# Expert 2's first layer split four slices later, and expert 0's low products three slices behind the high ones

## The chip, the cores and the metric

One core of one Trainium2 chip runs the kernel. The metric is the device time of one execution in microseconds (us); lower is better. The core has a matrix engine (TensorE, PE in the profile, its weight loads PEld), VectorE (DVE), ScalarE (ACT), GpSimd (POOL) and SyncE (SP), which work side by side, each through its own instructions in order, and 16 DMA engines.

## The reference

What is computed is an attention whose mask comes from hashed signs, followed by a layer of eight experts. Each token goes to the one expert with the largest gate logit:

```python
for i in range(N):                     # N = 1536 tokens of D = 512
    e = expert_idx[i]
    if counts[e] < capacity:           # capacity 384
        disp[e, counts[e]] = x[i]
        ...
h = np.maximum(np.einsum('ecd,edf->ecf', disp, w1), 0.0)   # w1: 8 x 512 x 1024
y = np.einsum('ecf,efd->ecd', h, w2)                       # w2: 8 x 1024 x 512
for i in range(N):
    if keep[i]:
        out[i] = gate_w[i] * y[expert_idx[i], pos[i]]
```

All of it is float32.

## The kernel before

The attention takes the first 250 us or so and isn't touched. After it the eight experts run one after another. An expert has up to two tiles of 128 tokens (more are dealt with in a branch behind a test, which is not taken in the execution profiled here). The hidden width of 1024 is cut into eight **slices** of 128, numbered f = 0 to 7.

To keep float32 accuracy on TensorE, each operand is split into a high part (rounded by ACT, names ending in h) and a low part (the rest, made by DVE, or for two slices by POOL, names ending in l). A product is then three matmuls: high by high, high by low, low by high. So each slice of a weight costs an ACT and a DVE instruction before its last matmul can run. `split1` and `split2` (by `split`, L1143 and L1144) do this for a slice of w1 and of w2, for the expert after the one that is being computed.

`layer1` (L1205) makes a slice of the hidden layer in 12 matmuls into one of three PSUM banks, in turn; `relu` (L1174 on ACT, L1175 on DVE) empties the bank into `hh` and `hl`; then it calls `each(f)`. So the fourth slice can't begin before the relu of the first has read its bank, and so on. `layer2` (L1222) adds up three matmuls for each slice and tile into one bank for each tile: `w2h` with `hh`, `w2l` with `hh`, `w2h` with `hl`, in this order, and calls `each(f)` after a slice. In the loop over the experts, `each1` (called in `layer1`) splits slice f of the next expert's w1 and, at odd f, loads a piece of two slices of the w1 of the expert after that; `each` (called in `layer2`) splits slice f of the next expert's w2, loads on, and at f = 3 turns the next expert's tokens with `prep_x` (transposes on PE at L1164, `xh` by ACT, `xl` by DVE).

Expert 0 is different. Its first tile is computed in `hidden` (raw float32, L178) between the last steps of the routing; its w2 is split by `split_hi` (ACT, L1244) and `split_lo` (DVE and POOL, L1250), and its hidden layer by `relu_hi` and `relu_lo` (L1260, L1264). Then come `layer2` for its first tile, in which `turn` (L1181) transposes its second tile after slice 6; `raw_layer1` (L178) for the second tile, during which expert 1's w1 (`r1x`) is split; and `layer2` for the second tile. From then on experts 1 to 7 follow.

What sets the order is the order in which this code is written: instructions go to each engine's queue as the code issues them, and each queue is worked through in that order. Loads of weights are issued on SP (`load_w1`, `load_w2`), those of expert 1's w1 and of most of its w2 on ACT's queue; gathers of tokens and scatters of results on POOL. A buffer of raw weights is loaded again when both parts of the split before it have been made.

Of the kernel before, what the change touches and what calls it, by code (L numbers as in the profile page):

```python
# [114 lines left out]
def hash_attention_moe(ctx, tc, qT, kT, vL, wg, w1, w2, cst, out, CAP):  # L115
    nc = tc.nc
# [37 lines left out]
    def load_w1(e, c):  # L154
        t = wr.tile([128, 2, 4, 128], F32, tag="r1", name=f"r1_{e}")
        nc.sync.dma_start(out=t, in_=w1[e, :, 2 * c:2 * c + 2])
        return t

    raw1, raw2, xg = {}, {}, {}
    def load_w2(e, c, t=None, q=nc.sync):  # L160
        raw2[e, c] = t or gp.tile([128, 2, 512], F32, tag="r2", name=f"r2_{e}", bufs=3)
        q.dma_start(out=raw2[e, c], in_=w2[e, :, 2 * c:2 * c + 2])
# [3 lines left out]
    def col(e, t):  # L166
        return NJ if t == 3 else 3 * e + t
# [945 lines left out]
    with tc.manual_schedule():  # L1113
# [16 lines left out]
        W1, W2 = {}, {}  # L1130

        def load_w1c(e, c):
            if e < E and (e, c) not in raw1:
                raw1[e, c] = load_w1(e, c)

        def next_w2(n):
            if n + 3 < 4 * E:
                load_w2(*divmod(n + 3, 4))
# [8 lines left out]
        def split1(e, f, eng=nc.vector):  # L1147
            W1[e, f] = split(raw1[e, f // 2][:, f % 2], "w1", eng)

        def split2(e, f, eng=nc.vector):  # L1150
            W2[e, f] = split(raw2[e, f // 2][:, f % 2], "w2", eng)

        def fetch(e, t):
            gather(e, t, gp.tile([128, XW], F32, tag="xr", name="xr"))

        def prep_x(e, t0, nt):
            W = 128 * nt
            xr = [xg.pop((e, t0 + t)) for t in range(nt)]
            xh = xp.tile([128, 4, W], F32R, tag="xh", name="xh")
            xl = xp.tile([128, 4, W], F32R, tag="xl", name="xl")  # L1160
            for t, x in enumerate(xr):
                pt = ps.tile([128, 4, 128], F32, tag=f"t{t}", name="pt")
                for k in range(4):
                    nc.tensor.transpose(pt[:, k], x[:, k * 128:(k + 1) * 128], ident)  # L1164
                c = slice(t * 128, (t + 1) * 128)
                nc.scalar.activation(out=xh[:, :, c], in_=pt, func=AF.Copy)
                nc.vector.tensor_tensor(out=xl[:, :, c], in0=pt, in1=xh[:, :, c].bitcast(F32), op=ALU.subtract)
            return xh, xl

        def new_h(W):  # L1170
            return [hp.tile([128, 8, W], F32R, tag=tag, name=tag) for tag in ("hh", "hl")]
# [14 lines left out]
        def raw_layer1(e, xt, each):  # L1186
            hh, hl = new_h(128)
            for f in range(8):
                ph = ps.tile([128, 512], F32, tag=f"h{f % 3}", name="ph")
                raw_one(ph[:, :128], e, f, xt, range(4))  # L1190
                relu(ph[:, :128], hh[:, f], hl[:, f])
                each(f)
            return hh, hl

        def layer1(e, xhl, each):
            xh, xl = xhl
            W = xh.shape[2]
            hh, hl = new_h(W)
            for f in range(8):
                ph = ps.tile([128, 512], F32, tag=f"h{f % 3}", name="ph")  # L1200
                wh, wl = W1.pop((e, f))
                n = 0
                for k in range(4):
                    for w, x in ((wh, xh), (wh, xl), (wl, xh)):
                        nc.tensor.matmul(ph[:, :W], w[:, k], x[:, k], start=(n == 0), stop=(n == 11))  # L1205
                        n += 1
                relu(ph[:, :W], hh[:, f], hl[:, f])
                each(f)
            return hh, hl

        def layer2(e, hhl, t0, view, each, steps, now=True):
            hh, hl = hhl
            late = []
            py = {}
            for f, ts in steps:
                wh, wl = W2[e, f]
                for t in ts:
                    if f == 0:
                        py[t] = ps.tile([128, 512], F32, tag=("y0", "acc")[t], name="py")
                    c = slice(t * 128, (t + 1) * 128)  # L1220
                    for n, (h, w) in enumerate(((hh, wh), (hh, wl), (hl, wh))):
                        nc.tensor.matmul(py[t], h[:, f, c], w, start=(f == 0 and n == 0), stop=(f == 7 and n == 2))  # L1222
                    if f == 7:
                        def fin(t=t):
                            y = yp.tile([128, 512], F32, tag="y", name="y")
                            j = col(e, t0 + t)
                            nc.scalar.activation(out=y, in_=py[t], func=AF.Copy, scale=gsc[:, j:j + 1])  # L1227
                            nc.gpsimd.indirect_dma_start(  # L1228
                                out=outv[view(t)], out_offset=bass.IndirectOffsetOnAxis(ap=yix[:, j:j + 1], axis=0),
                                in_=y, in_offset=None, bounds_check=out.shape[0] - 1, oob_is_err=False)  # L1230

                        if now:
                            fin()
                        else:
                            late.append(fin)
                each(f)
            return late
# [18 lines left out]
        h0 = new_h(128)  # L1256
# [44 lines left out]
        def each0(f):  # L1301
            if f == 6:
                last_gates(0)
                xg[0, 1, "T"] = turn(0, 1)

        fin = layer2(0, h0, 0, lambda t: 0, each0, [(f, (0,)) for f in range(8)], False)
        for c in range(3):
            load_w2(1, c, q=nc.scalar)

        def each1(f):  # L1310
            if f in (0, 3, 6):
                last_gates((0, 3, 6).index(f) + 1)
            if f == 4:
                fin[0]()
            split1(1, f)

        h1 = raw_layer1(0, xg.pop((0, 1, "T")), each1)
        both = [(f, (0, 1)) for f in range(8)]
        apart = [(f, (t,)) for t in range(2) for f in range(8)]
        nxt = {}  # L1320
        for e in range(E):
            more = e + 1 < E
            if more and e:
                fetch(e + 1, 0)
                fetch(e + 1, 1)

            def each1(f):
                if more:
                    split1(e + 1, f)
                    if f % 2 and e + 2 < E:  # L1330
                        load_w1c(e + 2, f // 2)

            if e:
                hhl = layer1(e, nxt.pop("xhl"), each1)

            def each(f):
                if more:
                    split2(e + 1, f)
                    if f % 2:
                        next_w2(4 * (e + 1) + f // 2)  # L1340
                    if e == 0 and f > 3:
                        load_w1c(2, f - 4)
                    if f == 3:
                        nxt["xhl"] = prep_x(e + 1, 0, 2)

            if e:
                layer2(e, hhl, 0, lambda t: 2 * e + t, each, both if more else apart)
            else:
                layer2(0, h1, 1, lambda t: 1, each, [(f, (0,)) for f in range(8)])
                nmax = nc.values_load(mcnt[0:1, 0:1], min_val=0, max_val=2 * S)  # L1350
        with tc.If(nmax > WB):
# [3 lines left out]
            for e in range(E):  # L1355
# [8 lines left out]
                for t in (2, 3) if e == 0 else (2,):  # L1364
                    kept = {f: W1[e, f] for f in range(8)}
                    fetch(e, t)
                    hhl = layer1(e, prep_x(e, t, 1), lambda f: None)
# [31 lines left out]
```

## Time and profile before

| | us |
|---|---|
| median of 3 runs | 459.41 (458.39 to 460.09) |
| the profiled execution | 457.68 |
| its span, first to last instruction | 455.80 |
| mean granted TensorE clock, as a share of 2.4 GHz | 0.972 |
| PE busy | 421.9 (93%) |
| DVE, ACT, POOL busy | 322.2, 304.3, 207.9 |

The profiled execution is 1.73 us below the median of the runs, and 1.88 us of it lie outside the span. All times of day below are us from the span's start. A row of a timeline gives an instruction's start, its duration, engine, line, operation, output and inputs, shape and count, and in brackets how long the engine sat idle before it and for whom it waited.

### The profile page before, as it was taken

The page shows a single profiled execution, that of the slowest core. Times are in us where ns is not written, and L with a number is a line of the kernel's source. Part 1 is how long each engine was busy: PE and PEld are TensorE (multiplying, and loading weights), DVE is VectorE, ACT ScalarE, POOL GpSimd, SP SyncE. Part 2 cuts the span into 40 slices and gives each one's busy share as a digit, 9 for nine tenths or more (in the row PEclk, how much of TensorE's full clock was granted, in tenths as well). Part 3 has the DMA queues.
Part 4 walks back from the last instruction along what each step waited for, and adds up shares of the span by engine and source line. Part 5 has one row for each costly group of instructions (what it writes and reads, how often), then busy time and mean ns, then how long its engine had stood idle before and what let it go on. Part 6 is the DMA issues. An engine that isn't in the chain of part 4 may idle for free. (4 is left out here: it accounts for less than half of the span.)

```text
span 455.8 us, 10104 instructions
## 1 busy us (share of the span) xinstructions
PE 421.9 (93%) x3891; PEld 359.5 (79%) x3891; DVE 322.2 (71%) x675; ACT 304.3 (67%) x467; POOL 207.9 (46%) x190
## 2 busy tenths in 40 slices
PE   7887999699989999899998999899999999999993
PEld 2565877488877887787887879789898989898982
DVE  3886899976887879899867478576657575756310
ACT  4278989679777989999893447556565665656310
POOL 7567666778785775586872330203030303030100
PEclk9998999889988999999989999999999999999997
DMA  8997989889978999998897894977676666751000
GB/s 204 268 204 141 187 179 216 204 180 156 213 156 165 174 199 180 185 227 181 163 143 185 288 327 152 364 264 242 204 230 223 217 231 205 248 174 47 36 1 33
DMA packets 98910, 86.59 MB, mean 190 GB/s; under 512 B 79266, under 2 KB 81282, under 8 KB 98856
## 3 DMA queue, kind: packets, MB, share of 16 engines
q1 hardware_dynamic: 95288, 74.87, 68.7%
q0 software_dynamic: 2560, 7.34, 4.8%
q10 hardware_dynamic: 1008, 3.67, 2.3%
q8 instruction: 32, 0.52, 0.5%
q14 instruction: 22, 0.18, 0.2%
HBM read 48.35 MB, written 7.34 MB: 122 GB/s over the span
## 5 line engine op out<-in xcount | busy, mean ns | idle before, releaser
L1228 POOL DMA_INDIRECT y<-y,yix x16 | 17.5, 1095 | 150.1 <-ACT y L1227 134.7
L692 POOL TENSOR_TENSOR p<-p,p 128x768 f16<-128x768 f32 x37 | 62.2, 1700 | 21.3 <-ACT p L778 14.5
L1205 PE MATMUL ph<-xh,w1h 128*128 128x256 f32 x224 | 63.6, 284 | 2.2 <-DVE hl L1175 2.2
L1205 PE MATMUL ph<-xl,w1h 128*128 128x256 f32 x224 | 63.4, 283 | 0.0
L1205 PE MATMUL ph<-xh,w1l 128*128 128x256 f32 x224 | 63.4, 283 | 0.0
L625 PE MATMUL pt<-KA,QA 128*128 128x512 f32 x192 | 59.0, 390 | 2.3 <-ACT p L774 1.0
L692 POOL TENSOR_TENSOR d<-p,d 128x768 f16<-128x768 f32 x27 | 48.5, 1807 | 23.0 <-ACT d L678 10.8
L625 PE MATMUL pt<-KB,QB 78*128 78x512 f32 x192 | 53.7, 363 | 4.5 <-DMA KB<-bits 3.3
L743 DVE TENSOR_REDUCE mx<-pt 128x1 f32<-128x768 f32 x48 | 45.2, 951 | 9.3 <-PE pt L625 8.8
L1144 DVE TENSOR_TENSOR w2l<-r,w2h 128x512 fp32r<-128x512 f32 x56 | 36.0, 686 | 21.9 <-ACT w2h L1143 21.9
L1222 PE MATMUL py<-w2l,hh 128*128 128x512 f32 x128 | 50.2, 392 | 1.3 <-DVE w2l L1250 1.1
L1222 PE MATMUL py<-w2h,hh 128*128 128x512 f32 x128 | 50.8, 397 | 0.3 <-ACT hh L1260 0.3
L1222 PE MATMUL py<-w2h,hl 128*128 128x512 f32 x128 | 50.1, 391 | 0.0
L774 ACT ACTIVATE p<-pt,lnb 128x768 f32<-128x768 f32 x48 | 42.4, 896 | 10.0 <-PE pt L625 4.4
L639 DVE TENSOR_REDUCE dm<-pt 128x1 f32<-128x768 f32 x48 | 45.4, 949 | 5.1 <-PE pt L625 4.8
L670 ACT ACTIVATE p<-pt,ds 128x768 f32<-128x768 f32 x48 | 47.1, 990 | 2.1 <-DVE p L692 0.4
L1205 PEld LDWEIGHTS ph<-xh,w1h 128*128 128x128 f32 x224 | 43.0, 192 | 2.8 <-DVE hl L1175 2.6
L1174 ACT ACTIVATE hh<-ph 128x256 fp32r<-128x256 f32 (+1 forms) x64 | 23.6, 369 | 29.4 <-PE ph L1205 27.3
L1205 PEld LDWEIGHTS ph<-xl,w1h 128*128 128x128 f32 x224 | 43.0, 192 | 0.3
L1205 PEld LDWEIGHTS ph<-xh,w1l 128*128 128x128 f32 x224 | 43.0, 192 | 0.0
L625 PEld LDWEIGHTS pt<-KB,QB 78*128 78x128 f32 x192 | 32.2, 206 | 11.1 <-DMA KB<-bits 2.7
L625 PEld LDWEIGHTS pt<-KA,QA 128*128 128x128 f32 x192 | 32.6, 208 | 10.1 <-ACT p L774 2.2
(215 smaller groups left out, 942.5 us busy)
## 6 DMA issues: line engine op xcount, KB each, us to landing
r<-w SPq DMA_DIRECT2D x55, 512.0 KB
QA<-KA SPq DMA_DIRECT2D x28, 192.0 KB
vraw<-vL SPq DMA_DIRECT2D x4, 768.0 KB
raw<-qT SPq DMA_DIRECT2D x14, 192.0 KB
raw<-kT SPq DMA_DIRECT2D x14, 192.0 KB
KB<-KA SPq DMA_DIRECT2D x14, 192.0 KB
KA<-QB SPq DMA_DIRECT2D x14, 192.0 KB
r1x<-w ACTq DMA_DIRECT2D x4, 512.0 KB
```

The lines of the kernel that those rows point to most:

```text
L625: nc.tensor.matmul(t[:, a:z], s[:K, q * 128:(q + 1) * 128], m[:K, a:z], start=(n == 0), stop=(n == 1))
L639: nc.vector.tensor_reduce(out=m, in_=tiles["d", k, t][:, 0:S], axis=AX.X, op=ALU.max, negate=True)
L670: nc.scalar.activation(out=p32_of("dp", k)[:, t], in_=pt_last("d", k, t), func=AF.Exp, scale=s[:, 0:1], bias=s[:, 1:2])
L692: eng.tensor_tensor(out=out[:, t], in0=p32[:, t], in1=p1[:, t], op=ALU.subtract)
L743: nc.vector.tensor_reduce(out=m[:, 0, q:q + 1], in_=pt_last("m", r, t), axis=AX.X, op=ALU.max)
L774: nc.scalar.activation(out=p32_of("rp", r)[:, t], in_=pt_last("e", r, t), func=AF.Exp, scale=0.125, bias=lnb)
L1144: eng.tensor_tensor(out=lo, in0=r, in1=hi.bitcast(F32), op=ALU.subtract)
L1174: nc.scalar.activation(out=hh, in_=ph, func=AF.Relu)
L1205: nc.tensor.matmul(ph[:, :W], w[:, k], x[:, k], start=(n == 0), stop=(n == 11))
L1222: nc.tensor.matmul(py[t], h[:, f, c], w, start=(f == 0 and n == 0), stop=(f == 7 and n == 2))
L1228: nc.gpsimd.indirect_dma_start(out=outv[view(t)], out_offset=bass.IndirectOffsetOnAxis(ap=yix[:, j:j + 1], axis=0), in_=y, in_offset=None, ...
```

## The change

Two edits. In `layer2` of expert 0's first tile (`lag` = 3), a slice's two products with the high part of w2 come first, and the product with the low part comes three slices later; the last slice takes all that are left. Then the loop over experts: for e = 1 alone, `each1` splits nothing at f = 0 to 3 and slices 0 to 3 of expert 2's w1 at f = 4 to 7; slices 4 to 7 are split in `layer2` of expert 1, one at each of f = 0 to 3, behind the slice of w2. The loads of expert 3's w1, which hang on these splits, move along. Nothing else changes, and no instruction is added or removed.

```diff
-        def layer2(e, hhl, t0, view, each, steps, now=True):
+        def layer2(e, hhl, t0, view, each, steps, now=True, lag=0):
...
-                    for n, (h, w) in enumerate(((hh, wh), (hh, wl), (hl, wh))):
-                        nc.tensor.matmul(py[t], h[:, f, c], w, start=(f == 0 and n == 0), stop=(f == 7 and n == 2))
+                    if lag:
+
+                        ops = [(hh, f, 0), (hl, f, 0)]
+                        ops += [(hh, g, 1) for g in ([f - lag] if f < 7 else range(7 - lag, 8)) if g >= 0]
+                    else:
+                        ops = [(hh, f, 0), (hh, f, 1), (hl, f, 0)]
+                    for n, (h, g, w) in enumerate(ops):
+                        nc.tensor.matmul(py[t], h[:, g, c], W2[e, g][w], start=(f == 0 and n == 0),
+                                         stop=(f == 7 and n == len(ops) - 1))
...
-        fin = layer2(0, h0, 0, lambda t: 0, each0, [(f, (0,)) for f in range(8)], False)
+        fin = layer2(0, h0, 0, lambda t: 0, each0, [(f, (0,)) for f in range(8)], False, 3)
...
-            def each1(f):
+            def first(f):
                 if more:
                     split1(e + 1, f)
                     if f % 2 and e + 2 < E:
                         load_w1c(e + 2, f // 2)
+
+
+            def each1(f):
+                if e != 1:
+                    first(f)
+                elif f > 3:
+                    first(f - 4)
...
+                    if e == 1 and f < 4:
+                        first(4 + f)
```

PE's queue at expert 0's first tile, slices 2 to 4 (`py` is the bank, the names after the arrow the slice's part of w2 and of the hidden layer). Before:

```order
L1222 MATMUL py_4618<-w2h_4473,hh_4459 128x512
L1222 MATMUL py_4618<-w2l_4597,hh_4459 128x512
L1222 MATMUL py_4618<-w2h_4473,hl_4460 128x512
L1222 MATMUL py_4618<-w2h_4511,hh_4459 128x512
L1222 MATMUL py_4618<-w2l_4599,hh_4459 128x512
L1222 MATMUL py_4618<-w2h_4511,hl_4460 128x512
L1222 MATMUL py_4618<-w2h_4513,hh_4459 128x512
L1222 MATMUL py_4618<-w2l_4601,hh_4459 128x512
```

After, from slice 2 until the low product of that slice, `w2l_4597`, comes up:

```order
L1227 MATMUL py_4618<-w2h_4473,hh_4459 128x512
L1227 MATMUL py_4618<-w2h_4473,hl_4460 128x512
L1227 MATMUL py_4618<-w2h_4511,hh_4459 128x512
L1227 MATMUL py_4618<-w2h_4511,hl_4460 128x512
L1227 MATMUL py_4618<-w2l_4564,hh_4459 128x512
L1227 MATMUL py_4618<-w2h_4513,hh_4459 128x512
L1227 MATMUL py_4618<-w2h_4513,hl_4460 128x512
L1227 MATMUL py_4618<-w2l_4566,hh_4459 128x512
L1227 MATMUL py_4618<-w2h_4515,hh_4459 128x512
L1227 MATMUL py_4618<-w2h_4515,hl_4460 128x512
L1227 MATMUL py_4618<-w2l_4597,hh_4459 128x512
```

The low product of slice 2 stood directly behind the slice's first product and now stands ten places behind it.

ACT's queue in expert 1's `layer1` (`hh_4911` is expert 1's hidden layer, `r1_2_4851` and `r1_2_4862` the first two raw pieces of expert 2's w1). Before:

```order
L1174 ACTIVATE hh_4911<-ph_4913 128x256
L1143 ACTIVATE w1h_4928<-r1_2_4851 128x512
L1174 ACTIVATE hh_4911<-ph_4932 128x256
L1143 ACTIVATE w1h_4947<-r1_2_4851 128x512
L1174 ACTIVATE hh_4911<-ph_4953 128x256
L1143 ACTIVATE w1h_4968<-r1_2_4862 128x512
L1174 ACTIVATE hh_4911<-ph_4972 128x256
L1143 ACTIVATE w1h_4987<-r1_2_4862 128x512
L1174 ACTIVATE hh_4911<-ph_4993 128x256
```

After:

```order
L1174 ACTIVATE hh_4911<-ph_4913 128x256
L1174 ACTIVATE hh_4911<-ph_4928 128x256
L1174 ACTIVATE hh_4911<-ph_4943 128x256
L1174 ACTIVATE hh_4911<-ph_4958 128x256
L1174 ACTIVATE hh_4911<-ph_4973 128x256
L1143 ACTIVATE w1h_4988<-r1_2_4851 128x512
L1174 ACTIVATE hh_4911<-ph_4992 128x256
L1143 ACTIVATE w1h_5007<-r1_2_4851 128x512
L1174 ACTIVATE hh_4911<-ph_5013 128x256
L1143 ACTIVATE w1h_5028<-r1_2_4862 128x512
```

Five relus now stand ahead of the first split of expert 2's w1. On ACT's queue of `layer2` that follows, the other four splits have come in between those of expert 2's w2, ahead of `prep_x`'s `xh`:

```order
L1143 ACTIVATE w2h_5061<-r2_2_4826 128x512
L1143 ACTIVATE w1h_5065<-r1_2_4871 128x512
L1143 ACTIVATE w2h_5075<-r2_2_4826 128x512
L1143 ACTIVATE w1h_5081<-r1_2_4871 128x512
L1143 ACTIVATE w2h_5093<-r2_2_4860 128x512
L1143 ACTIVATE w1h_5097<-r1_2_4887 128x512
L1143 ACTIVATE w2h_5107<-r2_2_4860 128x512
L1143 ACTIVATE w1h_5113<-r1_2_4887 128x512
L1166 ACTIVATE xh_5119<-pt_5121 128x4x128
```

Before, the four `w2h` rows stood there alone.

## Rows read from the trace of the kernel before

**Rows 1.** The page, granted clock in 40 slices, tenths of full speed.

```profile
PEclk9998999889988999999989999999999999999997
```

**Rows 2.** Stages: from:to, length, busy of PE, PEld, DVE, ACT, POOL, clock, DMA share, GB/s.

```profile
259.83:268.24 8.41, 7.04 (x28) 4.59 (x28) 5.90 (x18) 3.82 (x10) 5.90 (x5) 1.00 0.71 220
...
282.72:296.90 14.18, 12.03 (x98) 11.62 (x96) 8.13 (x16) 7.09 (x16) 3.06 (x3) 1.00 0.96 352
...
308.71:320.23 11.52, 11.52 (x98) 11.52 (x97) 8.05 (x15) 7.73 (x17) 4.28 (x4) 1.00 0.74 234
...
282.72:308.71 25.99, 23.84 (x154) 21.47 (x152) 15.91 (x29) 13.83 (x29) 3.06 (x3) 1.00 0.87 310
308.71:332.03 23.32, 23.32 (x154) 21.36 (x152) 15.11 (x26) 14.00 (x29) 4.28 (x4) 1.00 0.69 223
```

**Rows 3.** Who waited for whom, PE, 283 to 456: us, times, longest.

```profile
PE ph L1205 <- DVE hl L1175: 2.2, 2, 1.5
```

**Rows 4.** PE's timeline in expert 0's first tile, second layer.

```profile
259.83 0.50 PE L1222 MATMUL py<-w2h,hh 128*128 128x512 f32 x1 [0.28 <-ACT hh L1260]
...
260.56 0.50 PE L1222 MATMUL py<-w2h,hl 128*128 128x512 f32 x1
...
261.55 0.51 PE L1222 MATMUL py<-w2l,hh 128*128 128x512 f32 x1 [0.26 <-POOL w2l L1250]
...
263.60 0.50 PE L1222 MATMUL py<-w2l,hh 128*128 128x512 f32 x1 [1.07 <-DVE w2l L1250]
...
264.17 0.39 PE L1222 MATMUL py<-w2h,hh 128*128 128x512 f32 x1
...
266.90 0.60 PE L1181 MATMUL pt<-cs,xr 128*128 128x128 f32 x4
...
267.57 0.40 PE L1222 MATMUL py<-w2l,hh 128*128 128x512 f32 x1
...
268.24 3.84 PE L178 MATMUL ph<-xt,r 128*128 128x128 f32 x32
```

**Rows 5.** Timelines of DVE, POOL and ACT there; last the gather issued at 258.84, landing.

```profile
262.06 0.88 DVE L1264 SCALAR_TENSOR_TENSOR hl<-ph,hh 128x128 fp32r<-128x128 f32 x4 [1.55 <-ACT hh L1260]
262.86 1.28 DVE L1250 TENSOR_TENSOR w2l<-r,w2h 128x512 fp32r<-128x512 f32 x2
264.06 1.89 DVE L1250 TENSOR_TENSOR w2l<-r2x,w2h 128x512 fp32r<-128x512 f32 x3
...
261.46 1.28 POOL L1250 TENSOR_TENSOR w2l<-r2x,w2h 128x512 fp32r<-128x512 f32 x1
...
262.39 0.65 ACT L1244 ACTIVATE w2h<-r2x 128x512 fp32r<-128x512 f32 x1
...
xr<-xd,gix POOLq DMA_INDIRECT x1, 3.9
```

**Rows 6.** Weight loads in 259.8 to 268.2: busy us, mean ns, idle before.

```profile
L1222 PEld LDWEIGHTS py<-w2l,hh 128*128 128x128 f32 x8 | 1.5, 188 | 2.4 <-DVE w2l L1250 1.5 <-POOL w2l L1250 0.7
```

**Rows 7.** What follows: DVE's timeline, and ACT's DMA queue in 261 to 267 (packets, MB).

```profile
269.81 0.29 DVE L1175 SCALAR_TENSOR_TENSOR hl<-ph,hh 128x128 fp32r<-128x128 f32 x1 [2.29 <-ACT hh L1174]
...
281.29 1.28 DVE L1167 TENSOR_TENSOR xl<-pt,xh 128x512 fp32r<-128x512 f32 x2
...
q10 hardware_dynamic: 301, 1.12, 63.8%
```

**Rows 8.** Expert 1's first layer on PE and ACT; last expert 2's gather of 288.07, landing.

```profile
290.11 0.39 PE L1205 MATMUL ph<-xh,w1h 128*128 128x256 f32 x1 [1.48 <-DVE hl L1175]
...
288.37 0.63 ACT L1143 ACTIVATE w1h<-r 128x512 fp32r<-128x512 f32 x1 [2.45 <-DMA r<-w]
...
294.84 0.63 ACT L1143 ACTIVATE w1h<-r 128x512 fp32r<-128x512 f32 x1 [0.97 <-DMA r<-w]
...
297.16 0.63 ACT L1143 ACTIVATE w1h<-r 128x512 fp32r<-128x512 f32 x1 [0.62 <-DMA r<-w]
...
xr<-xd,gix POOLq DMA_INDIRECT x1, 7.9
```

More of the change, by code (lines that the diff above doesn't have):

```diff
@@ L1215, in layer2 @@
             for f, ts in steps:
-                wh, wl = W2[e, f]
                 for t in ts:
```

## The prediction, made before the changed kernel had run

> **What bounds the kernel now.** I read the waits of PE first, then a table of stages, then the timelines of the two places that the edits touch. From 283 us to the end PE waits for another engine just twice, 2.2 us in all [rows 3]; otherwise the last 173 us are PE's alone, so whatever makes PE reach that stretch earlier moves the end by as much. Both waits lie in expert 1's first layer. The table shows it: experts 1 and 2 do the same work, yet expert 1 takes 25.99 us and expert 2 takes 23.32; the first layers alone are 14.18 and 11.52 [rows 2]. Before that, expert 0's first tile spends 8.41 us in its second layer, of which PE is busy 7.04 [rows 2], with two marked waits for low parts of w2, 0.26 and 1.07 us [rows 4].
>
> **Edit 1: the low products of expert 0's first tile, three slices later.** The same 24 matmuls and 4 transposes remain; only waits can go. First the prices. Between 264.17 and 266.90 twelve matmuls run without a wait, so one takes 2.73 / 12 = 0.2275 us. From 263.60, just after a wait, two take 0.57, 0.11 more than two at that pace: a restart. From the transposes at 266.90 to the second matmul behind them it is 0.67, so the transposes cost 0.67 - 0.2275 = 0.44 [rows 4].
>
> Now the new order. The first high product still starts at 259.83. Behind it now comes the product with hl, which before stood third and began at 260.56 [rows 4]; it can't begin sooner, since that part is what it waited for. The low product that filled this gap goes elsewhere. From 260.56 there are 23 matmuls, one restart and the transposes: 260.56 + 0.11 + 23 x 0.2275 + 0.44 = 266.34, if nothing waits. Is everything there in time? With k matmuls behind 260.67, a place starts at 260.67 + 0.2275 k. Slice 4's hl product (k = 9) starts at 262.72; its four hl are made from 262.06 in steps of 0.22, the first by 262.3. The low products of slices 2 and 3 (k = 13, 16) start at 263.63 and 264.31; DVE ends them near 263.54 and at 264.14. The second tile's transposes fall at 264.54; their gather has landed by 258.84 + 3.9 = 262.7. The last hi split ends at 263.04, for a place at 264.98. The last low products (slices 4 to 7, k = 19 to 22, 0.44 for the transposes added) start from 265.43 on, slice 7's at 266.12; POOL has made slice 4's at 262.74, and DVE ends the last at 265.95 [rows 5]. The narrowest margins, 0.09 to 0.17 us, are thin, but a miss costs only its own size. Raw layer 1, which starts at 268.24 [rows 4], can start at 266.34, and its ACT copy of the transposed tile has the six last matmuls as cover. **Gain 1.90.** Bounds: the two marked waits less one matmul that the hl wait now leaves uncovered, 1.33 - 0.23 = 1.1; and 2.1 if the first hl comes for free.
>
> A rule that speaks against the edit: before, the high and the low product of a slice stood side by side and share the operand hh; now they stand apart. In this stage the rows have eight weight loads for the eight `w2l,hh` products, 188 ns each, 1.5 us together [rows 6]: hh was loaded again every time, so nothing shared is lost. The Trainium skill, "TensorE: Matmul & The Clock Gate", Part 2, says weights may stay put over many matmuls, to "load once and matmul repeatedly". By that, parting the two would cost up to eight loads, and edit 1 would gain 0.4 rather than 1.9; the trace has no such sharing to lose, so it stays out of the sum and is rival (5).
>
> Does the gain reach expert 1? What follows is bound closely by DVE: the low part of expert 1's tokens (`xl`) ends at 281.29 + 1.28 = 282.57 [rows 7], and expert 1's first layer starts at 282.72 [rows 2]. So DVE must move too. Its run of work begins at 269.81 with the relu of raw layer 1, after 2.29 us idle for ACT, which waits for PE [rows 7]: DVE can begin 1.90 earlier. Expert 1's w1, split in that run, comes through ACT's DMA queue: by 267.0 it had moved 301 packets and 1.12 MB, two of the four half-megabyte pieces [rows 7], and the first piece would be wanted at about 267.8. The loads behind it on SP are released by DVE's splits, and move along.
>
> **Edit 2: expert 2's w1 split four slices later.** Before, ACT's in-order queue put a split of expert 2's w1 behind each relu, and four of these splits waited for their load, the first 2.45 us, until 288.37, the last until 297.16 [rows 8]. The relus stood behind them, so PE had no free bank: 1.48 us before 290.11 [rows 8], 0.7 later. With five relus ahead of the first split, the three banks turn over freely. A slice takes 11.52 / 8 = 1.44; with edit 1 the first layer starts at 280.82, the fifth slice is done at 288.0, and the first split comes at about 288.4, when its load was there in the old trace already. PE's last slice needs the bank of the fifth, whose relu is ahead of all splits: PE waits for none. **Gain 14.18 - 11.52 = 2.66.** Bounds: 2.2, the marked waits without restarts, and 2.67 by the whole expert.
>
> Where the splits go: four to relus 5 to 8, four into expert 1's second layer (280.82 + 11.52 = 292.34 to 304.15, with expert 2's own 11.81 = 23.32 - 11.52 us). There the third of them waits for the load that came at 297.16. Behind it on ACT stand two splits and `xh`; behind those on DVE `xl`, which expert 2's first layer waits for. Counting from 297.16 three splits and two `xh` at 0.63 and 1.28 for `xl`: 301.6, against 304.15. On DVE, nine splits of 0.63 from about 293.2, then `xl`, end at 300.2. PE's transposes at 297.8 find a gather that had landed by 288.07 + 7.9 = 296.0 even unmoved [rows 8]. So the cover is 2.5 us. On SP, expert 2's last w2 piece now goes ahead of two pieces of expert 3's w1; these are wanted only in the first layer that starts at 304, and DMA falls from a share of 0.96 to 0.74 by then [rows 2]. POOL's queue doesn't change.
>
> **The sum.** 1.90 + 2.66 = 4.56. The profiled execution of 457.68 would be 453.1; the median lies 1.73 above it, so 459.41 - 4.56 = **454.9**. PE's clock gives nothing back or away: granted at full speed (2.4 GHz) in both stages, gaps included [rows 1, 2].
>
> **Rivals.** (1) *DVE or the loads hold expert 1's start.* For it: only 0.15 us lie between `xl` and PE's start. Against: DVE's run begins with 2.29 us of idle that edit 1 removes. If expert 1 still starts at 282.72, edit 1 gives nothing: 459.41 - 2.66 = 456.8. (2) *The load wait returns.* If the first pieces of expert 2's w1 come later than 288.4, the sixth relu waits behind its split as before. For it: DMA is at a share of 0.96 and 352 GB/s there [rows 2]. Against: the piece was there at 288.37, and only three relus remain exposed, of which PE needs none. Up to all of edit 2: 457.5. (3) *Neither works*, as PE's end is held by something the trace hides: 459.4. Against: PE's unbroken work from 308.71 on. (4) *Slower.* The place is `prep_x` of expert 2: with L the landing of the last w1 piece, its first layer can't start before L + 4.4 (above). From L = 304.3 the change loses; L = 307 would give a start of 311.4 instead of 308.71, 462.1. It takes a load 10 us later than 297.16, while its issue moves earlier: little speaks for it. (5) *Parting the two products costs a weight load each.* Eight loads of 188 ns come off edit 1: 456.4. Against: those eight are in the rows already [rows 6].
>
> **Chances and range.** Forecast 0.75, (1) 0.11, (2) 0.07, (3) 0.03, (4) 0.03, (5) 0.01. The forecast's own range: up by 0.8 (edit 1 at 1.1) and 0.5 (edit 2 at 2.2), down by 0.2, and some 0.8 either way for the median of a few runs (458.39 to 460.09 before). With rival (1) inside I give 453.8 to 457.0. 0.5% of the time, 2.3 us, is about what a measurement of this kernel tells from no change, so the line is at 457.1: faster 0.85 (the forecast, most of (1), a little of (2)), same 0.12, slower 0.03.
>
> **What would show it.** Right: raw layer 1 starting near 266.3; expert 1's first layer near 280.8 and 11.5 us long, with no PE wait for `hl`; expert 1 in 23.3 us, and the rest shifted by 4.6. Rival (1) shows as a wait of PE for `xl`; (2) as the old wait two or three slices later; (4) as a wait ahead of expert 2's first layer. The forecast is wrong if any of these is over 1 us, or if a low product of slices 2, 3 or 7 makes PE wait.

## The result, and the profile after

| | before | after |
|---|---|---|
| median of 6 executions each, us | 458.48 (457.44 to 460.09) | 451.58 (450.18 to 455.68) |
| ratio after / before | | 0.9857, 95% interval 0.9818 to 0.9896 |
| the profiled execution (span), us | 457.68 (455.80) | 450.18 (448.3) |

The changed kernel is faster by 6.9 us in the medians (4.8 to 8.3 by the interval). The forecast was 454.9 with a range of 453.8 to 457.0, so the direction came out and the time lies 2.2 us below the range. The ratios leave out executions more than 1.5% above the fastest of their kernel (none here, six of twelve in edit1_only below); means, where they are given, take in all.

A trace below is the profile of one execution. The same views as before. The page's granted clock, in 40 slices:

```profile
PEclk9598999999989989999998999999999999999997
```

The table of stages (from:to, length, busy of PE, PEld, DVE, ACT, POOL, clock, DMA share, GB/s): expert 0's first tile, second layer, then expert 1's first layer, expert 1 whole, expert 2 whole.

```profile
256.58:263.51 6.93, 6.59 (x32) 4.91 (x30) 5.35 (x13) 3.65 (x10) 6.20 (x5) 1.00 0.77 236
277.88:289.39 11.51, 11.51 (x97) 11.51 (x96) 6.96 (x14) 5.76 (x13) 3.07 (x3) 1.00 0.98 336
277.88:301.20 23.32, 23.32 (x154) 21.36 (x152) 16.47 (x29) 14.06 (x29) 3.07 (x3) 1.00 0.95 317
301.20:324.52 23.32, 23.32 (x154) 21.36 (x152) 15.02 (x26) 13.95 (x29) 4.39 (x4) 1.00 0.76 253
```

Against [rows 2], 8.41 became 6.93, 14.18 became 11.51 and expert 1 takes what expert 2 takes. The waits of PE from 256 us to the end (for whom, us, times, longest) are down to one row, where [rows 3] had two waits and [rows 4] two more:

```profile
PE py L1227 <- DVE w2l L1256: 0.2, 1, 0.2
```

The wait stands in PE's timeline of expert 0's first tile at the low product of slice 2:

```profile
256.58 0.48 PE L1227 MATMUL py<-w2h,hh 128*128 128x512 f32 x1
257.17 0.50 PE L1227 MATMUL py<-w2h,hl 128*128 128x512 f32 x1
...
260.02 0.39 PE L1227 MATMUL py<-w2h,hl 128*128 128x512 f32 x1
260.64 0.50 PE L1227 MATMUL py<-w2l,hh 128*128 128x512 f32 x1 [0.23 <-DVE w2l L1256]
260.98 0.39 PE L1227 MATMUL py<-w2h,hh 128*128 128x512 f32 x1
...
261.68 0.60 PE L1181 MATMUL pt<-cs,xr 128*128 128x128 f32 x4
...
263.51 3.73 PE L178 MATMUL ph<-xt,r 128*128 128x128 f32 x32
```

From one product to the next it is 0.23 us, so the low product was due at 260.25 and started 0.39 late, with another 0.11 for the restart behind it. In ACT's timeline of expert 1 the splits of expert 2's w1 wait for no load any more, and `prep_x` comes with time to spare, as forecast:

```profile
285.55 0.62 ACT L1143 ACTIVATE w1h<-r 128x512 fp32r<-128x512 f32 x1
...
290.91 0.62 ACT L1143 ACTIVATE w1h<-r 128x512 fp32r<-128x512 f32 x1
...
294.04 0.62 ACT L1143 ACTIVATE w1h<-r 128x512 fp32r<-128x512 f32 x1
...
295.50 1.09 ACT L1166 ACTIVATE xh<-pt 128x512 fp32r<-128x512 f32 x2 [0.84 <-PE pt L1164]
```

Where did the 7.5 us between the two profiled executions go? From the first product to the end it is 195.97 us before (455.80 - 259.83) and 191.72 after (448.30 - 256.58): 4.25 us, made of 1.59 up to expert 1's start, 2.67 in its first layer and nothing behind. The other 3.25 us lie ahead of the first product, in code that neither edit touches. So two questions remain. Does the change act on that part? And is 4.25 what the touched part gives in other executions?

### The profile page after: what moved, and what is told of

Read it like the earlier page. It is cut to its first block, busy times and chain, and to the rows that moved or that the text cites. A ratio compares the mean times of both kernels' runs of the same rounds, so it can differ in the third digit from the quotient of the medians.

```text
span 448.3 us, 10103 instructions
## 1 busy us (share of the span) xinstructions
PE 415.6 (93%) x3891; PEld 357.0 (80%) x3891; DVE 324.0 (72%) x675; ACT 304.7 (68%) x467; POOL 208.8 (47%) x190
## 5 line engine op out<-in xcount | busy, mean ns | idle before, releaser
L692 POOL TENSOR_TENSOR p<-p,p 128x768 f16<-128x768 f32 x37 | 63.5, 1736 | 20.1 <-ACT p L778 12.1
L625 PE MATMUL pt<-KA,QA 128*128 128x512 f32 x192 | 57.4, 381 | 2.3 <-ACT p L774 0.9
L625 PE MATMUL pt<-KB,QB 78*128 78x512 f32 x192 | 52.5, 356 | 3.1 <-DMA KB<-bits 1.5
L1175 DVE SCALAR_TENSOR_TENSOR hl<-ph,hh 128x256 fp32r<-128x256 f32 (+1 forms) x64 | 25.9, 406 | 19.6 <-ACT hh L1174 16.6
```

What stands on the lines that cost most here:

```text
L625: nc.tensor.matmul(t[:, a:z], s[:K, q * 128:(q + 1) * 128], m[:K, a:z], start=(n == 0), stop=(n == 1))
L692: eng.tensor_tensor(out=out[:, t], in0=p32[:, t], in1=p1[:, t], op=ALU.subtract)
L1175: nc.vector.scalar_tensor_tensor(out=hl, in0=ph, scalar=0.0, in1=hh.bitcast(F32), op0=ALU.max, op1=ALU.subtract)
```

## The edits apart, and one of them in another place

Two theories. A: the edits act only where they stand; the time ahead of the first product differs from execution to execution, and the medians of a few runs carry that. B: the changed program also makes the part ahead of it faster (through its code, its loads or the buffers' places). To tell them apart I ran each edit alone; edit 2 at expert 4 instead of expert 1, where the rows show no wait to remove (so that it changes the program alike and should gain nothing); and both edits again.

**edit1_only** is the changed kernel with the loop over the experts as before.

```diff
-                if e != 1:
-                    first(f)
-                elif f > 3:
-                    first(f - 4)
+                first(f)
...
-                    if e == 1 and f < 4:
-                        first(4 + f)
```

> Only the low products of expert 0's first tile come three slices later; expert 2's w1 is split where it was. Theory A (the change acts in the expert stage alone, and the rest of the measured gain is the attention's own spread from execution to execution): from the first product of that layer to expert 1's first layer 21.3 us instead of 22.89, expert 1's first layer still about 14.2 with its two waits for hl, total 1.6 us below before. Theory B (any change of the program makes the attention ahead of it 2 to 3 us faster, by where code and data lie): the same in the expert stage, but the first product starts near 256.6 to 257.6 instead of 259.8 and the total is about 4 us below before. Rival 1 of the prediction (expert 1's start is held by DVE): no gain in the total.

Measured: 457.22 us (12 executions), ratio 0.9915 (0.9860 to 0.9971).

**edit2_only** is the changed kernel without the lag.

```diff
-        fin = layer2(0, h0, 0, lambda t: 0, each0, [(f, (0,)) for f in range(8)], False, 3)
+        fin = layer2(0, h0, 0, lambda t: 0, each0, [(f, (0,)) for f in range(8)], False)
```

> Only expert 2's w1 is split four slices later; the products of expert 0's first tile stand as before. Theory A: expert 1's first layer 11.5 us instead of 14.18, no PE wait for hl, expert 0's first tile still 8.4 us, total 2.7 us below before. Theory B: the same, and the total about 5 us below before, with the first product of expert 0's second layer near 256.6 to 257.6. Rival 2 (the load wait comes back later): 12.5 us or more in expert 1's first layer or a wait ahead of expert 2's.

Measured: 455.72 us (12), ratio 0.9925 (0.9887 to 0.9963).

**move_at_expert4** is edit2_only with the move at expert 4.

```diff
-                if e != 1:
+                if e != 4:
...
-                    if e == 1 and f < 4:
+                    if e == 4 and f < 4:
```

> The second edit applied to expert 4 instead of expert 1 (expert 5's w1 is split four slices later), the first edit not at all. PE waits for nothing in expert 4, so the expert stage has nothing to gain: 195.97 us from the first product of expert 0's second layer to the end, as before. Theory A: total as before, within 0.3%. Theory B: the program has changed as much as in the edit to expert 1, so the attention is 2 to 3 us faster and the total with it.

Measured: 456.93 us (12), ratio 0.9986 (0.9941 to 1.0031).

**both_again** is the changed kernel.

> The changed kernel once more. Theory A: from the first product of expert 0's second layer to the end 191.7 us again, total 4.3 us below before give or take the attention's spread (about 1 us on the median). Theory B: total 6 to 7 us below before again, and the first product of expert 0's second layer again near 256.6.

Measured: 452.35 us (6), ratio 0.9846 (0.9793 to 0.9899).

The kernel before had a median of 458.39 us beside these four, over 29 executions from 451.98 to 464.19. Over all executions the means lie below that of before by 1.5 us (edit1_only), 2.9 (edit2_only), 1.0 (move_at_expert4) and 5.7 (both_again), with standard errors of 0.8 to 1.1. Stage windows again, of edit1_only, edit2_only and both_again; the first row of each is expert 0's stage, the second expert 1's first layer:

```profile
263.08:269.96 6.88, 6.64 (x31) 4.92 (x30) 5.26 (x13) 3.81 (x10) 6.14 (x5) 1.00 0.72 209
284.33:299.98 15.65, 13.27 (x98) 13.06 (x97) 8.69 (x17) 7.53 (x17) 3.06 (x3) 0.89 0.94 350
```

```profile
261.75:270.48 8.73, 6.96 (x32) 4.57 (x30) 6.25 (x18) 3.58 (x10) 6.15 (x5) 1.00 0.81 270
284.96:296.47 11.51, 11.51 (x98) 11.51 (x97) 6.95 (x14) 5.74 (x13) 3.05 (x3) 1.00 0.98 339
```

```profile
261.12:268.05 6.93, 6.57 (x31) 4.90 (x30) 5.51 (x13) 3.48 (x10) 6.21 (x5) 1.00 0.76 247
282.39:293.90 11.51, 11.51 (x97) 11.50 (x96) 6.98 (x14) 5.76 (x13) 3.06 (x3) 1.00 0.98 350
```

Each edit does its work in its own stage, alone as well as with the other, to within 0.05 us. Theory B finds no support. The move at expert 4 gains nothing that its interval can tell (by its lower end it could still be 2.7 us), and the first product came at 263.08 and 261.75 us in the kernels with one edit and at 261.12 in a second trace of both, later than in the kernel before (259.83). On the mean of five traces of the kernel before it came at 258.3, on the mean of the five with both edits (three of them are variants described further on) at 259.3. Over all fourteen traces of this study it lies between 255.6 and 263.1 us, with the same code ahead of it. An execution thus carries some 3 to 4 us either way before the change is even reached.

The trace of move_at_expert4 missed its expectation of 195.97 us from the first product to the end: it took 198.97. Experts 4 and 5 took 23.3 us each as before; the 3 us lie in the two stages that its edit leaves alone, expert 0's first tile (10.26) and expert 1's first layer (15.28).

Edit 1 alone shows something else: its trace gained 1.53 us in the first stage (8.41 to 6.88) and lost 1.47 in expert 1's first layer (14.18 to 15.65). PE's one wait there is longer. Expert 1 comes 1.6 us sooner behind the first product, but the load ahead of the first split, which holds the relus, only 0.7, so ACT waits longer for it than the 2.45 us of [rows 8]:

```profile
PE ph L1205 <- DVE hl L1175: 2.4, 1, 2.4
...
290.88 0.63 ACT L1143 ACTIVATE w1h<-r 128x512 fp32r<-128x512 f32 x1 [3.45 <-DMA r<-w]
```

And the clock in that layer is 0.89. This is what the next runs are about.

## What PE's clock does after a wait

The forecast had the clock at full speed through both stages, gaps included, as the one trace of before showed [rows 1, 2]. To see whether that holds I profiled the kernel before four more times.

> The kernel before, unchanged, looked at once more. Theory C (PE's two waits that the change removes cost a different amount in every execution, by the landing of the loads and by a stretch of half clock that may follow a wait; the profile on which the prediction rests showed a cheap case): from the first product of expert 0's second layer to the end anything from 195.9 to 199 us, with its first stage between 8.4 and 10.3 and expert 1's first layer between 14.1 and 15.7, while expert 2 on take 147.1 us as ever. Theory A (these stages are as in the first profile, and the rest of the gain is attention's spread): 195.97 within 0.2.

> The same kernel, another look. Theory C: another value in 195.9 to 199 us for the expert stage, differing from the last look's; with a half-clock stretch between 258 and 300 us in one of such looks or more. Theory A: 195.97 within 0.2 again.

> The kernel before, a further look, for the mean of its expert stage. Looks so far, from the first product of expert 0's second layer to the end: 195.97, 197.18, 195.58, and 198.97 in the kernel that moves expert 5's splits. Theory C: again between 195.5 and 199; together the looks lie on average 5 us or more above the changed kernel's 191.7. Theory A: 195.97.

> As the look before it: theory C 195.5 to 199 us for the expert stage and another value than in that look, theory A 195.97.

| trace | first product at | to raw layer 1 | to expert 1 | expert 1's first layer | first product to end |
|---|---|---|---|---|---|
| before [rows 2] | 259.83 | 8.41 | 22.89 | 14.18 | 195.97 |
| before_look_a | 257.40 | 8.70 | 23.17 | 15.09 | 197.18 |
| before_look_b | 258.75 | 8.44 | 22.92 | 13.76 | 195.58 |
| before_look_c | 257.16 | 8.42 | 22.90 | 15.07 | 196.87 |
| before_look_d | 258.24 | 8.48 | 22.96 | 14.07 | 195.95 |
| after | 256.58 | 6.93 | 21.30 | 11.51 | 191.72 |
| both_again | 261.12 | 6.93 | 21.27 | 11.51 | 191.69 |

(The executions were 456.46, 456.12, 455.91 and 456.06 us for a to d.) Only before_look_d fits theory A. Two of the five traces of the kernel before have a stretch at half clock in expert 1's first layer. Windows of before_look_c, the layer and that stretch, and its wait and the first products about it:

```profile
280.06:295.13 15.07, 13.29 (x98) 13.08 (x97) 8.68 (x17) 7.20 (x16) 3.06 (x3) 0.89 0.95 348
289.20:292.60 3.40, 3.40 (x19) 3.40 (x18) 1.91 (x4) 2.14 (x5) 0.00 (x0) 0.50 1.02 414
```

```profile
287.75 0.39 PE L1205 MATMUL ph<-xh,w1h 128*128 128x256 f32 x1 [1.78 <-DVE hl L1175]
...
290.19 0.41 PE L1205 MATMUL ph<-xl,w1h 128*128 128x256 f32 x1
290.40 0.41 PE L1205 MATMUL ph<-xh,w1l 128*128 128x256 f32 x1
```

After 1.78 us without work and another 1.5 of work, the clock falls to 1.2 GHz for 3.4 us: products come every 0.21 us there and not every 0.12 (11.52 / 96), and PE is busy 13.29 us with the layer that it otherwise does in 12.03 [rows 2]: 1.26 us more. The 12.03 hold two waits, each of which adds 0.26 to the busy time ((12.03 - 11.51) / 2), and this layer has one, so the clock's own share is about 1.5. The same happened in edit1_only (293.10 to 296.50) and, in expert 0's stage, in move_at_expert4, whose profiled execution took 10.26 us there:

```profile
263.90:267.30 3.40, 3.40 (x10) 2.69 (x9) 3.07 (x11) 0.00 (x0) 1.70 (x2) 0.50 0.94 313
```

But move_at_expert4 also has the longest wait of all these traces, and no such stretch behind it. In its expert 1's first layer PE waited 2.56 us, and the clock stayed at full speed:

```profile
284.00:299.28 15.28, 12.01 (x97) 11.59 (x96) 8.72 (x17) 7.42 (x17) 3.05 (x3) 1.00 0.97 350
...
292.47 0.39 PE L1205 MATMUL ph<-xh,w1h 128*128 128x256 f32 x1 [2.56 <-DVE hl L1175]
```

None of the traces of the changed kernel, or of the one with a lag of four below, has such a stretch in these stages. That a wait brings the slow stretch is so far only seen side by side, and not in every case, so I tried to take away the idleness and leave the waits.

**waits_filled** is the kernel before with matmuls of zeros, which add nothing to any result, in the four places where PE waits.

```diff
+                if e == 1 and W == 256 and f in (4, 6):
+                    warm_pe(pg, 7 if f == 4 else 4)
...
+                        if not now and n == 1 and f in (1, 2):
+                            warm_pe(pg, (0, 1, 5)[f])
```

> The kernel before with matmuls of zeros into an unused bank put where PE waits: 1 and 5 of 128x512 (about 0.22 us each) ahead of the low products of slices 1 and 2 of expert 0's first tile, 7 and 4 ahead of slices 4 and 6 of expert 1's first layer. They fit into the waits of 0.42, 1.24, 1.6 and 0.95 us, so they cost nothing, and the waits themselves stay. Theory C with the clock as its main part: PE is busy throughout, no half-clock stretch falls between 258 and 300 us, first stage about 8.4 and expert 1's first layer about 14.2 or as late as the loads land; total 1 to 2 us below before on the median. If the loads' landing is the main part of the spread, expert 1's first layer still varies and the total stays at before. Theory A: total as before, within 0.3%.

Measured: 457.85 us (12), ratio 1.0042 (1.0004 to 1.0079), no half clock in the two stages of its trace. As a test it failed. In the first stage the filling brought a wait of its own, since its matmuls write a bank that expert 0's hidden layer was still using:

```profile
262.50 0.38 PE L182 MATMUL pg<-wz 128*128 128x512 bf16 x1 [1.70 <-DVE hl L1268]
```

The stage took 9.74 us and expert 1's first layer 14.96, so what the clock may have given back is not to be read from it. I then went the other way and added waits to the changed kernel, in layers where there are none.

**waits_added** puts nine copies into ACT's queue ahead of the second slice's relu, in the first layers of experts 2 to 7; they write a buffer that nobody reads any more.

```diff
+                if e > 1 and W == 256 and f == 1:
+                    for _ in range(9):
+                        nc.scalar.activation(out=xt0.rearrange("p k c -> p (k c)"), in_=wz, func=AF.Copy)
```

> The changed kernel with nine idle copies of 128x512 put on ACT in each first layer of experts 2 to 7, ahead of the second slice's relu, so that PE waits about 2 us (9 x 0.52 less the 2.6 us that the three banks cover) before slice 4 of each: six waits of the size of those that the change took away, where the changed kernel has none. Theory C (a wait of PE is followed by a stretch of half clock in some cases, which costs about 1.5 us more): two or more of the six experts show a half-clock stretch of 3.4 us right behind the wait, and take 26.5 to 27.5 us instead of 23.3; the others take 25.4. Theory A (the clock doesn't go by these waits): six equal experts of 25.4 us at full clock.

**waits_added_filled** has these copies too, and nine matmuls of zeros in the wait that they make, into a bank of their own.

```diff
+                if e > 1 and W == 256 and f == 4:
+                    warm_pe(ps.tile([128, 512], F32, tag="acc", name="pw"), 9)
```

> The same with nine matmuls of zeros (128x512, about 0.22 us each) on PE ahead of slice 4 of these six first layers, into a bank that is free: PE is busy for nearly all of each wait, and the wait itself stays. Theory C: no half-clock stretch from 300 us on, six equal experts of about 25.4 us. If half clock comes all the same, it goes not by PE's idleness but by something else in these stages (ACT's extra work, for one).

Measured: 487.24 and 469.39 us, one execution each. PE's waits (us, times, longest) in waits_added, and in waits_added_filled:

```profile
PE ph L1205 <- DVE hl L1175: 18.8, 6, 3.2
```

```profile
PE ph L1207 <- DVE hl L1175: 7.1, 6, 1.3
```

One expert's window of waits_added, with the half-clock stretch in it, and one of waits_added_filled:

```profile
306.89:335.17 28.28, 25.06 (x154) 22.89 (x152) 14.57 (x26) 19.29 (x38) 4.27 (x4) 0.94 0.62 208
317.41:320.81 3.40, 3.40 (x18) 3.40 (x17) 2.15 (x5) 1.42 (x5) 0.00 (x0) 0.51 0.68 214
```

```profile
326.99:353.79 26.80, 25.54 (x163) 22.21 (x161) 14.56 (x26) 19.17 (x38) 4.27 (x4) 1.00 0.59 192
```

All six waits of waits_added are followed by half clock, four times for 3.4 us and twice for 6.8; an expert with 3.4 us of it takes 28.28 us (28.11 in one of four). In waits_added_filled ACT is held up just as long, but PE works on zeros for most of the time: no stretch at half clock, and 26.80 us for an expert. So of the 4.96 us that an added wait costs (28.28 - 23.32), 3.48 are the wait (26.80 - 23.32) and **1.48 the clock**, and it is PE's idleness that brings the clock down, not the late data. This is shown for these waits, five of 3.2 us and one of 2.7; they came out longer than the 2 us that were meant, and longer than those of before. For the waits of before it remains a matter of single traces: three layers with one wait of 1.8 to 2.4 us were followed by half clock, three with two shorter ones (the longest 1.1 to 1.7) were not, and neither was the one with 2.56 and 0.71. In expert 0's stage waits of 0.73 and 0.84 were followed by it in move_at_expert4, and waits of 0.78 to 0.90 in before_look_a and edit2_only were not. So the length of a wait alone doesn't decide; what else does, no run here shows.

The Trainium skill, "TensorE: Matmul & The Clock Gate", Part 1, has two levels of the clock, 1.2 and 2.4 GHz, and idleness as what brings the lower one. The rows above agree on both (0.50 against 1.00, and the zeros that keep it up).

## The one wait that is left, and a lag of four

In both traces of the changed kernel, and in the two with added waits, slice 2's low product waits for DVE, 0.23 to 0.24 us by its row. DVE's and POOL's timelines of the changed kernel show why; the first row is POOL's second low part, the other two are DVE's five low parts, two and three in a row:

```profile
258.73 1.31 POOL L1256 TENSOR_TENSOR w2l<-r2x,w2h 128x512 fp32r<-128x512 f32 x1
...
259.44 1.75 DVE L1256 TENSOR_TENSOR w2l<-r,w2h 128x512 fp32r<-128x512 f32 x2
261.11 1.88 DVE L1256 TENSOR_TENSOR w2l<-r2x,w2h 128x512 fp32r<-128x512 f32 x3
```

Two of them took 1.75 us where [rows 5] have 1.28 for two. The first one alone took 1.15 us and the second 0.68, and POOL was at its own low part for the first 0.60. In the trace of before, POOL's ended at 262.74 and DVE's first began at 262.86 [rows 5]: they didn't meet. Over the traces the time follows the overlap:

| trace | POOL still busy for, us | DVE's first low part, us |
|---|---|---|
| before, before_look_c, before_look_d, lag_of_four | 0 | 0.68 to 0.75 |
| before_look_a | 0.42 | 0.97 |
| after | 0.60 | 1.15 |
| both_again | 0.78 | 1.33 |
| waits_added | 1.22 | 1.77 |

In the last four rows DVE ends 0.55 us behind POOL however early it began: all of its work but the first 0.13 us (0.68 - 0.55) waits until POOL's instruction is through. The traces that the table leaves out fit: an overlap of 0.13 us cost nothing (before_look_b), and with 0.36 to 0.84 us DVE ended 0.56 behind POOL (edit1_only, edit2_only, move_at_expert4, waits_added_filled). No run moved POOL's instruction on purpose, so this is read from traces side by side. In the traces of the first row PE's first product had waited 0.25 to 0.64 us for ACT's relu, in those of the other rows not at all: the one trace that the forecast had was of the kind in which the two don't meet. The Trainium skill, "SBUF — State Buffer", section "Who interferes with whom", says that a DVE instruction with two inputs in SBUF contends with a GpSimd instruction that reads SBUF, and that the second to issue is blocked until the first is through. The rows agree; the forecast had counted DVE and POOL as independent.

**lag_of_four** puts the low products four slices behind instead of three, which gives slice 2's another 0.68 us.

```diff
-        fin = layer2(0, h0, 0, lambda t: 0, each0, [(f, (0,)) for f in range(8)], False, 3)
+        fin = layer2(0, h0, 0, lambda t: 0, each0, [(f, (0,)) for f in range(8)], False, 4)
```

> The changed kernel with the low products four slices behind instead of three. In the changed kernel's profile the low product of slice 2 still waited 0.23 us for DVE, 0.4 us with the restart. All theories: that wait goes, from the first product to raw layer 1 6.5 us instead of 6.93, unless the low parts at the end come too late, and total 0.4 us below the changed kernel, which is less than these runs can tell.

Measured: 451.28 us (12), ratio 0.986 (0.9822 to 0.9897). Its stage:

```profile
262.10:268.72 6.62, 6.39 (x28) 4.94 (x29) 5.00 (x13) 3.82 (x10) 4.71 (x4) 1.00 0.77 249
```

The wait is gone and the stage is 0.31 us shorter, 191.41 us from the first product to the end against 191.7. That isn't proof for the lag: in this trace PE's first product was held up by ACT for 0.64 us, POOL was ahead, and DVE's part took 0.68. What speaks for it is its place: slice 2's low product now comes 4.33 us behind the first product, and in the four traces where that wait showed it could start at 4.06 to 4.07. By the whole time the two kernels can't be told apart.

waits_added also showed that edit 1 has made another wait possible. The second tile's transposes, now earlier, met a gather that landed 6.7 us after its issue and not 3.9 as in [rows 5]:

```profile
267.33 0.66 PE L1181 MATMUL pt<-cs,xr 128*128 128x128 f32 x4 [1.00 <-DMA xr<-xd,gix]
```

In that trace raw layer 1 began 8.16 us behind the first product, and nearly all of edit 1's gain was gone. Five traces had both edits (with a lag of three or four), and this was the only one with that wait.

## Why the prediction was wrong

**Edit 2: right.** 14.18 - 11.51 = 2.67 against 2.66 forecast; no wait of PE for `hl`, no load ahead of the splits, `prep_x` in time, experts 2 to 7 unchanged. Alone it gave 2.67 by its trace against the mean of the five traces of before (196.31 - 193.64); that these agree so closely is luck, since it is 2.92 in its own stage (14.43 - 11.51) less 0.24 in a first stage that happened to be long (8.73 against 8.49).

**Edit 1: the mechanism right, the size too large.** 1.48 us to raw layer 1 and 1.59 to expert 1, inside the bounds of 1.1 to 2.1, not 1.90. Of the 6.93 us, 6.51 were forecast (266.34 - 259.83). The product with hl came 0.14 earlier than counted (0.59 behind the first product and not 0.73), and slice 2's low product cost 0.39 and a restart of 0.11. The margin of 0.09 us, which the text called thin, was overrun because POOL blocked DVE; the text had named a wait there as a sign of being wrong. Expert 1 did come earlier by the whole gain, so rival (1) did not occur; nor did (2) to (5).

**The sum: right for the part that the edits touch.** Over five traces of before and two of after, the stretch from the first product to the end is 196.31 - 191.70 = 4.6 us shorter, against 4.56. That it agrees is luck in part, for two errors cancel in it: edit 1 gave 1.68 on the mean (22.97 - 21.29), 0.2 less than forecast, and edit 2's stage gave 2.92, 0.3 more, since in two of the four further traces of before that layer took 0.9 us longer than in the one that I had.

**Two steps failed.** The first is "PE's clock gives nothing back or away: granted at full speed (2.4 GHz) in both stages, gaps included". One trace can't say that. In two of five traces a wait of before was followed by 3.4 us at half clock. Those two layers took 15.08 us on the mean and the other three 14.00, which is 0.4 on the mean of five; taking out the waits takes that out with them.

The second, and the larger, is the level: "the median lies 1.73 above it, so 459.41 - 4.56", with "some 0.8 either way for the median of a few runs". The 0.8 came from three executions (458.39 to 460.09). The 59 executions of the kernel before that were timed beside others have a median of 457.9 and reach from 452 to 464; the part ahead of the change, whose end lies between 255.6 and 263.1 us by the traces, moves them by several us. The 35 of them that ran beside the changed kernel have a median of 458.4 (the other 24 ran beside later runs, 23 of them with a median of 456.8). With that level the same sum gives 458.4 - 4.6 = 453.8, the lower bound of the range. One execution spreads by 2.1 to 2.5 us (standard deviation of the 12 of the changed kernel and of these 59). A median of three is then uncertain by about 1.25 x 2.3 / 1.73 = 1.7 us and a median of six by 1.25 x 2.3 / 2.45 = 1.2, which makes 2.0 from one to the other and not 0.8. The forecast was 3.3 us off (454.9 - 451.6).

About 1.0 of this is the level (459.4 against 458.4). The other 2 us, down to the 12 executions of the changed kernel (median 451.8), are not explained by any run here. Their mean lies 6.0 us below that of the 35, with a standard error of 0.7, so that 4.6 is 1.9 errors away. On the mean the traces place no more than 4.6 in the part that the edits touch, and don't show the part ahead of it faster with both edits (259.3 against 258.3). That it is draw from the attention is the likeliest reading, and argued, not shown.

## What to carry to other kernels

A change in one stage can be forecast to a few tenths from one trace, yet the level of the whole can't: look at how far the untouched part varies over several executions before giving a range. Removing a wait of TensorE can give more than the wait, as in some executions a slow stretch of its clock follows it. A margin of a tenth of a microsecond on DVE is none where POOL works on the same kind of operands at that moment.

## What was not expected of the hardware

- The clock fell to half for 3.4 us after single waits of 1.78 to 2.4 us, about 1.5 us of loss each, but not after one of 2.56. After added waits of 2.7 to 3.2 us it fell six times in six (1.48 us for 3.4 us of it); with zero matmuls in the wait it stayed up.
- DVE's 128x512 subtraction from SBUF took 0.68 us alone and up to 1.77 while POOL ran one, ending 0.55 us behind POOL's.
- A gather of 128 rows landed 3.9 us after issue in one trace and 6.7 in another, at the same place of the program.
- The same 256 us of code ahead of the change took from 255.6 to 263.1 us.
